# Reordering the end of the first attention stage and the start of the first product on TensorE

## Chip, cores, metric

One NeuronCore of one Trainium2 chip runs the whole program. The metric is the device time of one execution in microseconds (us).

## The reference

Attention over 8 batches, 12 heads, 448 tokens, head size 64, with normalised queries and keys; its output, viewed as 3584 rows of 768, goes through a two-layer product with a "snake" activation.

```python
def _attn_ref(q, k, v, g_q, g_k):
    q_n, k_n = rmsnorm(q, g_q), rmsnorm(k, g_k)
    # ... scale = 1 / sqrt(head size) ...
    scores = scale * np.matmul(q_n, k_n.transpose(0, 1, 3, 2))
    # ... softmax over the keys, which gives attn ...
    # ... attn times v is returned ...

def _moe_ref(x, w_in, w_out, alpha):
    h = x @ w_in                      # 768 -> 2048
    s = np.sin(alpha * h)
    g = h + s * s / (alpha + 1e-09)
    return g @ w_out                  # 2048 -> 768
```

## The kernel before

For each batch the kernel works through 6 pairs of heads in 3 chunks. A chunk has 7 score tiles (`scores`, one exponential each on ScalarE); a pair has 7 key tiles of values (`attend`), then a reciprocal on ScalarE (a logarithm and an exponential) and a division on VectorE that writes the pair's rows of `xT`. Then the first product makes 16 h tiles, each from 6 rows of weights, row `kt` needing pair `kt`'s division. From the second batch on, attention is interleaved with the second product of the batch before. The first batch has nothing to interleave with, so its waits are visible. The change touches only the end of that first stage.

PSUM, the memory that TensorE writes its results to, is given out as four pairs of banks. A new tile takes the pair that a predicted clock says comes free first, and waits for the last reader of what was in it. Fillers are matmuls on blank data whose results nobody uses:

```python
    def bank_pair(name, dtype=F32):
        slot = min(free_at, key=free_at.get)
        clock["pe"] = max(clock["pe"], free_at.pop(slot))
        ps = psum.tile([P, 2, 2048 // mybir.dt.size(dtype)], dtype, tag=f"ps{slot}", name=name)
        # ...
    def scores(c, j, warm=0):
        sc = bank_pair("sc")
        for _ in range(warm):                     # fillers on blank data
            nc.tensor.matmul(sc[:, 0], blank[:, :P], blank, start=True, stop=True)
        # ... 4 matmuls of 64*64 ...
        nc.scalar.activation(expT[c, j], sc[:, :, :S], ACT.Exp, scale=SCALE)

    def attend(pi, tiles=range(NJ)):
        if tiles[0] == 0:
            avs[pi] = bank_pair("av")
        # ... 4 matmuls of 64*64 for each key tile ...
        if tiles[-1] < NJ - 1:
            return
        nc.scalar.activation(rec, av[:, 1, :S], ACT.Ln)
        nc.scalar.activation(rec, rec, ACT.Exp, scale=-1.0)
        for hi in range(2):
            # ...
            nc.vector.tensor_mul(xT[b][r, hp, :], av[r, 0, :S], rec[o, :])

    def first_product(b, beside):
        # ...
        EARLY = 2
        tiles = {i: bank_pair("hps") for i in range(EARLY)}
        for kt in range(KT):
            for m in range(2 * EARLY):
                mm(tiles[m // 2], m, [kt])
        for i in range(MT // 2):
            if i >= EARLY:
                tiles[i] = bank_pair("hps")
                # ... 6 rows for each of 2 h tiles ...
            # ... snake of the two h tiles, then:
            for task in beside.get(i, ()):
                task()

    # end of the first stage; S_ = next score tile, A_ = values of the next pair (pairs 2 to 5 here)
    S_(1), A_(), S_(1), S_(1), S_(), A_(), S_()
    c4.reduce(0), c4.reduce(1)      # sums of squares of the fifth chunk, VectorE
    A_(2)                           # pairs 4 and 5, last key tiles last
    c4.rsqrt()
    # ... beside: c3.pe_transpose at 0, i.e. after the first two h tiles
    first_product(0, beside)
```

## Time and profile before

| | before |
|---|---|
| time, median of 3 | 436.57 us |
| span of the profiled execution | 434.7 us |
| TensorE busy | 98% |
| share of TensorE in the chain that ended last | 81% |
| first product of batch 0 starts | 39.05 us |
| its last 72 matmuls start | 45.18 us |

The waits and the timeline of the stretch are shown in the prediction. One line was not read closely enough before predicting. It is in the timeline of weight loads (start, length, engine, line, operation, operands, count, idle time before and its releaser) of the kernel before:

```profile
45.18 2.00 PEld L353 LDWEIGHTS <-w_in 128*128 128x128 bf16 x12
47.56 1.44 PEld L353 LDWEIGHTS <-w_in 128*128 128x128 bf16 x9 [0.38 <-DVE qkT L276]
```

In this trace weight loads run ahead of the matmuls, and a wait of theirs need not appear as idle matmul time: the second row has 0.38 us of it, the row of the 72 matmuls shows none. After 12 matmuls the load for the seventh h tile waits for VectorE's copy of the transposes, whose bank pair it inherits.

### The profile page before, as it was taken

The page shows a single profiled execution, that of the slowest core. Times are in us where ns is not written, and L with a number is a line of the kernel's source. Part 1 is how long each engine was busy: PE and PEld are TensorE (multiplying, and loading weights), DVE is VectorE, ACT ScalarE, POOL GpSimd, SP SyncE. Part 2 cuts the span into 40 slices and gives each one's busy share as a digit, 9 for nine tenths or more (in the row PEclk, how much of TensorE's full clock was granted, in tenths as well). Part 3 has the DMA queues.
Part 4 walks back from the last instruction along what each step waited for, and adds up shares of the span by engine and source line. Part 5 has one row for each costly group of instructions (what it writes and reads, how often), then busy time and mean ns, then how long its engine had stood idle before and what let it go on. Part 6 is the DMA issues. An engine that isn't in the chain of part 4 may idle for free.

```text
span 434.7 us, 9516 instructions
## 1 busy us (share of the span) xinstructions
PE 423.9 (98%) x3845; PEld 220.8 (51%) x3845; DVE 231.4 (53%) x335; ACT 338.5 (78%) x529; POOL 279.5 (64%) x263
## 2 busy tenths in 40 slices
PE   7889999999999999999999999999999999999996
PEld 3345554555455555555555555555555555555563
DVE  4787564557355564547454564464645474246511
ACT  5888789878888787878879788887878788788600
POOL 4968789936995559927798369946599176002300
PEclk9999999999999999999999999999999999999999
DMA  7999999691259704692067903494063901320022
GB/s 254 208 260 211 211 189 237 163 210 45 65 151 218 145 0 126 126 239 84 8 195 186 188 1 81 149 226 121 1 192 89 126 1 33 85 57 2 0 67 79
DMA packets 68240, 54.63 MB, mean 126 GB/s; under 512 B 39636, under 2 KB 63972, under 8 KB 68196
## 3 DMA queue, kind: packets, MB, share of 16 engines
q1 hardware_dynamic: 54834, 40.51, 36.6%
q0 software_dynamic: 12416, 11.81, 18.1%
q10 hardware_dynamic: 946, 1.70, 1.0%
q8 instruction: 30, 0.49, 0.5%
q14 instruction: 14, 0.11, 0.1%
HBM read 45.62 MB, written 11.01 MB: 130 GB/s over the span
## 4 chain that ended last, share of the span: by engine, by line
PE 81%; POOL 2%; DMA 1%; DVE 1%; issue 1%
PE ops L400 32%; PE hps L353 29%; PE av L314 13%; PE sc L294 7%; DMA qkT<-qkn 1%; POOL sq L221 1%; POOL qkn L246 1%; POOL qk L224 0%; DVE osb L406 0%; DVE xT L326 0%; DVE ms L227 0%
## 5 line engine op out<-in xcount | busy, mean ns | idle before, releaser
L297 ACT ACTIVATE expT<-sc 128x896 bf16<-128x896 f32 x168 | 144.6, 913 | 29.3 <-PE sc L294 28.3
L400 PE MATMUL ops<-w_out_sb,g_sb 128*128 128x384 bf16 x896 | 156.6, 327 | 0.0
L353 PE MATMUL hps<-xT,w_in 128*128 128x448 bf16 x768 | 147.3, 353 | 0.4 <-DVE xT L326 0.4
L335 POOL TENSOR_TENSOR s<-s 128x448 f32<-128x448 f32 x64 | 59.4, 932 | 115.0 <-ACT s L332 100.1
L400 PEld LDWEIGHTS <-g_sb 128*128 128x128 bf16 x896 | 83.1, 98 | 70.0 <-issue 18.8
L340 DVE SCALAR_TENSOR_TENSOR g_sb<-s,inv_alpha_sb,hps 128x448 bf16<-128x448 f32 x128 | 80.9, 677 | 62.1 <-POOL s L335 62.1
L353 PEld LDWEIGHTS <-w_in 128*128 128x128 bf16 x768 | 74.3, 98 | 72.3 <-issue 3.7
L332 ACT ACTIVATE s<-hps,alpha_sb 128x448 f32<-128x448 f32 x128 | 74.4, 627 | 28.9 <-PE hps L353 27.4
L326 DVE TENSOR_TENSOR xT<-av,rec 64x448 bf16<-64x448 f32 x96 | 59.7, 622 | 51.6 <-ACT rec L321 32.3
L246 POOL TENSOR_TENSOR qkn<-qk,inv 128x448 bf16<-128x448 f32 x80 | 72.6, 937 | 7.4 <-POOL qk L224 7.0
L221 POOL TENSOR_TENSOR sq<-qk 128x896 f32<-128x896 f32 x44 | 73.3, 1682 | 0.0
L314 PE MATMUL av<-expT,vb 64*64 64x448 bf16 x672 | 69.0, 349 | 1.2 <-ACT expT L297 0.8
L314 PE MATMUL av<-expT,ones 64*64 64x448 bf16 x672 | 69.1, 349 | 0.0
L227 DVE TENSOR_REDUCE ms<-sq 128x14 f32<-128x896 f32 x44 | 47.4, 1082 | 24.9 <-POOL sq L221 24.6
L406 DVE COPY osb<-ops 128x768 f32<-128x768 f32 (+1 forms) x33 | 27.6, 836 | 51.4 <-PE ops L400 45.5
L294 PE MATMUL sc<-qkT 64*64 64x448 bf16 x672 | 50.9, 361 | 1.7 <-DVE qkT L276 1.4
L224 POOL TENSOR_TENSOR qk<-qk,gg 128x896 f32<-128x896 f32 x24 | 50.1, 2090 | 1.7 <-ACT gg L171 1.7
L314 PEld LDWEIGHTS <-vb 64*64 64x64 bf16 x672 | 37.9, 107 | 13.4 <-issue 1.9
L314 PEld LDWEIGHTS <-ones 64*64 64x64 bf16 x672 | 37.1, 107 | 11.2
L337 ACT ACTIVATE s<-s 128x448 f32<-128x448 f32 x64 | 36.9, 577 | 2.7
L294 PEld LDWEIGHTS <-qkT 64*64 64x64 bf16 x672 | 14.9, 105 | 29.5 <-issue 26.2
L320 ACT ACTIVATE rec<-av 128x448 f32<-128x448 f32 x48 | 26.2, 545 | 4.0 <-PE av L314 3.5
(44 smaller groups left out, 140.8 us busy)
## 6 DMA issues: line engine op xcount, KB each, us to landing
qk<-in_q_dram SPq DMA_DIRECT2D x24, 448.0 KB, 4.3
qk<-in_k_dram SPq DMA_DIRECT2D x22, 448.0 KB, 5.2
out_dram<-osb SPq DMA_DIRECT2D x39, 192.0 KB, 2.8
vb<-in_v_dram POOLq DMA_DIRECT2D x32, 168.0 KB, 6.6
w_in<-in_moe_w_in_dram POOLq DMA_DIRECT2D x4, 768.0 KB, 11.8
w_out_sb<-in_moe_w_out_dram POOLq DMA_DIRECT2D x2, 1536.0 KB, 24.5
out_dram<-osb SPq DMA_DIRECT2D x26, 96.0 KB, 4.2
qk<-in_k_dram ACTq DMA_DIRECT2D x2, 448.0 KB, 5.9
```

Source lines behind the costliest of these rows:

```text
L221: nc.gpsimd.tensor_mul(st.sq[w], qk[ci][:, w], qk[ci][:, w])
L224: eng.tensor_mul(qk[ci][:, 0], qk[ci][:, 0], gg.to_broadcast([P, 2 * NJ, D]))
L246: eng.tensor_mul(n[:, :, hi, :], x[:, hi], inv[:, hi].unsqueeze(2).to_broadcast([P, NJ, D]))
L294: nc.tensor.matmul(sc[key_rows(pp, hi), pp, :S], qkt[r, 1, j * REST:(j + 1) * REST], qkt[r, 0, :], start=True, stop=True)
L297: nc.scalar.activation(expT[c, j], sc[:, :, :S], ACT.Exp, scale=SCALE)
L314: nc.tensor.matmul(av[o, part, :S], ones[r, :] if part else vb[b][r, hp, j, :], expT[pi // 2, j][r, pi % 2, :], start=(j == 0), stop=(j == ...
L326: nc.vector.tensor_mul(xT[b][r, hp, :], av[r, 0, :S], rec[o, :])
L332: nc.scalar.activation(s1, hps, ACT.Sin, scale=alpha_sb[:, m, :])
L335: nc.gpsimd.tensor_mul(s2, s1, s1)
L340: nc.vector.scalar_tensor_tensor(g_sb[:, m, (b % 2) * S:(b % 2 + 1) * S], s2, inv_alpha_sb[:, m, :], hps, op0=ALU.mult, op1=ALU.add)
L353: nc.tensor.matmul(ps[:, m % 2, :S], w_in_sb[m * 2 // MT][:, kt, m % (MT // 2) * P:(m % (MT // 2) + 1) * P], x[:, kt, :], start=(kt == 0), ...
L400: nc.tensor.matmul(st["ps"][:, k, :HALF], g_sb[:, m, c0:c0 + P], w_out_sb[:, m, half * HALF:(half + 1) * HALF], start=(m == 0), stop=(m == ...
```

## The change

Its intent is to remove TensorE's waits at the end of the stage: pair 3's reciprocal is held back so that the four last exponentials go first on ScalarE; the fifth chunk's sums leave the place in front of the last divisions; the first product does three rows of two h tiles before it needs a second bank pair, and puts the transposes where it would wait for the last division.

The diff, shortened (a helper that `A_(2)` used is dropped too):

```diff
         EARLY = 2
         tiles = {i: bank_pair("hps") for i in range(EARLY)}
-        for kt in range(KT):
+        for i in range(EARLY):
+            for m in (2 * i, 2 * i + 1):
+                mm(tiles[i], m, range(KT // 2))
+        for kt in range(KT // 2, KT):
+            if kt == KT - 1:
+                for task in beside.get(-1, ()):
+                    task()
             for m in range(2 * EARLY):
                 mm(tiles[m // 2], m, [kt])
@@
-    S_(1), A_(), S_(1), S_(1), S_(), A_(), S_()
+    S_(), A_()
     c4.reduce(0), c4.reduce(1)
-    A_(2)
+    attend(3, range(NJ - 1))
+    S_(), S_(), S_(), S_()
+    attend(3, [NJ - 1])
+    for last in (range(NJ - 1), [NJ - 1]):
+        for pi in (4, 5):
+            attend(pi, last)
     c4.rsqrt()
     beside = beside_h(0)
-    for i, task in ((0, lambda: c3.pe_transpose((0, 1))), (2, lambda: c4.scale(0, [0])), ...
+    for i, task in ((-1, lambda: c3.pe_transpose((0, 1))), (2, lambda: c4.scale(0, [0])), ...
```

More of the change, by code (lines that the diff above doesn't have):

```diff
@@ L472, in stage @@
         pairs = deque(b * NP + p for p in range(NP))
-        def values(n=1):
-            if n == 1:
-                return attend(pairs.popleft())
-            for js in (range(NJ - 1), [NJ - 1]):
-                for pi in list(pairs)[:n]:
-                    attend(pi, js)
-        return (lambda warm=0: scores(*tiles.popleft(), warm)), values
+        return (lambda warm=0: scores(*tiles.popleft(), warm)), (lambda: attend(pairs.popleft()))
     S_, A_ = stage(0)
@@ L521 @@
     load_qk(NC + 3)
-    S_(1), A_(), S_(1), S_(1), S_(), A_(), S_()
+    S_(), A_()
     c4.reduce(0), c4.reduce(1)
-    A_(2)
+    attend(3, range(NJ - 1))
[4 more added lines that the diff above has]
+            attend(pi, last)
     c4.rsqrt()
     beside = beside_h(0)
-    for i, task in ((0, lambda: c3.pe_transpose((0, 1))), (2, lambda: c4.scale(0, [0])), (3, lambda: c4.scale(0, [1])), (4, lambda: c4.scale(1, [0])),
+    for i, task in ((-1, lambda: c3.pe_transpose((0, 1))), (2, lambda: c4.scale(0, [0])), (3, lambda: c4.scale(0, [1])), (4, lambda: c4.scale(1, [0])),
                     (5, lambda: c4.scale(1, [1])), (6, step_of(NC + 1, 6)), (6, beside[3].pop())):
```

## The prediction

> **What bounds the kernel.** I read the page's busy shares and chain first, then the waits of TensorE between 25 and 46 us (the first batch's attention and the start of its first product), then the timelines of each engine there.
>
> ```profile
> PE 423.9 (98%) x3845; PEld 220.8 (51%) x3845; DVE 231.4 (53%) x335; ACT 338.5 (78%) x529; POOL 279.5 (64%) x263
> PEclk9999999999999999999999999999999999999999
> PE 81%; POOL 2%; DMA 1%; DVE 1%; issue 1%
> ```
>
> The matmul engine is busy in 98% of 434.7 us, at its full clock, and carries 81% of the chain that ended last. Only 10.8 us of it are idle, more than half of them before 35 us (29.1 busy of 35.0). The change touches a stretch of about 14 us that is executed once, so at best it can win the bubbles and the idle-time fillers of that stretch. These are the waits of TensorE there:
>
> ```profile
> PE sc L290 <- ACT expT L297: 1.1, 2, 0.8
> PE av L314 <- ACT expT L297: 0.6, 1, 0.6
> PE hps L353 <- DVE xT L326: 0.4, 1, 0.4
> ```
>
> The two last lie in the changed code. In the timeline (start, length, engine, line, operation, count, wait) they look so:
>
> ```profile
> 32.64 0.39 PE L290 MATMUL sc<-blank 128*128 128x512 bf16 x1
> ...
> 33.27 0.39 PE L290 MATMUL sc<-blank 128*128 128x512 bf16 x1
> ...
> 34.76 0.38 PE L314 MATMUL av<-expT,vb 64*64 64x448 bf16 x2 [0.59 <-ACT expT L297]
> ...
> 38.80 2.08 DVE L227 TENSOR_REDUCE ms<-sq 128x14 f32<-128x896 f32 x2
> ...
> 39.05 4.09 PE L353 MATMUL hps<-xT,w_in 128*128 128x448 bf16 x20
> ...
> 40.91 2.54 DVE L326 TENSOR_TENSOR xT<-av,rec 64x448 bf16<-64x448 f32 x4
> ...
> 43.51 0.92 PE L353 MATMUL hps<-xT,w_in 128*128 128x448 bf16 x4 [0.37 <-DVE xT L326]
> ...
> 44.36 0.89 PE L269 MATMUL tp<-ident,qkn 64*128 64x64 bf16 x28
> ...
> 45.18 13.91 PE L353 MATMUL hps<-xT,w_in 128*128 128x448 bf16 x72
> ```
>
> The reader sees fillers on blank data, a wait for an exponential, then the first product started at 39.05 with the operands of pairs 0 to 4. VectorE spends 2.08 us on the fifth chunk's sums just when the divisions of pairs 4 and 5 come due. The last pair's operand is ready at 43.45, so the last four matmuls of the first h tiles start at 43.51 instead of 42.91 (20 x 0.193 after 39.05): 0.60 us lost, of which the wait shows 0.37, the rest being drain. The transposes, ready since 33.4, stand behind them in the queue. From 45.18 to 66 us TensorE has no wait. So **45.18 is the mark**: how much earlier the 72 matmuls start is the gain.
>
> **What the Trainium skill says.** "TensorE: Matmul & The Clock Gate", section Back-to-back issue gap: N/2.4 + 2.5 ns, 189 ns for 448 columns; the trace has (13.91 - 0.35)/71 = 0.191, so it agrees. The same page, Part 2, step 1: only weight loads are pulled ahead, matmuls stay in program order; the transposes held up until 44.36 agree. "TensorEngine Tiling", Key Properties: "Changing tiling mode (not just tile) drains the TensorE"; going from 64*64 value matmuls to 128*128 ones costs 0.10 us here (the last value matmuls start at 38.76, their 0.19 end at 38.95, the next begins at 39.05), so it agrees. The clock page's table in "Why this matters for your kernels" allows no idle gaps over about 3 us; the stretch holds gaps up to 0.76 us at an unchanged clock, so shorter ones don't show it wrong.
>
> **The change part by part.** The instruction order of both kernels, laid side by side, differs in this stretch alone; afterwards only two PSUM bank pairs have exchanged names. TensorE loses three fillers (6 rows), everything else is moved. From the timeline I use: a key tile of values 0.19 (so 1.32 for seven, 1.13 for six), a tile of scores 0.19 to issue and 0.38 to finish, exponentials 0.90 alone and 0.82 in sequence, one logarithm plus exponential of a pair 1.1, one division 1.26 on VectorE, a semaphore 0.05. PSUM is given out as four pairs of banks, so a tile waits for the last reader of the pair that it inherits.
>
> Fillers. Each costs its 0.21 and two mode switches: from the end of the values at 32.51 to the scores at 32.96 are 0.45. The first (30.38) is worth nothing, as the values behind it wait until 31.19 for the second pair's division (29.88 + 1.26). The other two are 0.9 us of issue, but behind them stood the 0.59 wait for exponentials anyway.
>
> New order from 32.51, same until there. Six tiles of pair 3: 32.51 to 33.64. Scores 18 and 19: 33.64 to 34.02. ScalarE has finished pair 2's reciprocal and starts exponential 18 at 34.10 (scores done 34.02, 0.08 later), to 35.00; score tile 20 needs the same bank pair, so **it waits until 35.05**: about 1 us of new stall (0.85 visible). Score tile 21 needs the bank pair of pair 2, which VectorE frees at 35.20: 35.25. Exponentials 19, 20, 21 end at about 35.78, 36.60, 37.42. Last tile of pair 3: to 35.63. Pair 4 starts when exponential 19 frees its bank pair, 35.83; five tiles to 36.77, its sixth to 36.96; six of pair 5, 38.09; the two last tiles, 38.47. With the 0.10 switch the first product starts at **38.57 rather than 39.05: 0.48 earlier**.
>
> The chain of the divisions. Pair 3's logarithm is now behind exponential 21 on ScalarE: it starts at 37.40, reciprocal ready 38.55 (before: 37.48, so **1.07 later**). Pair 4's values finish at 38.44, reciprocal 39.65; pair 5's 40.69. The sums on VectorE now run at 35.20 to 36.27 and, since GpSimd's second square ends at 36.60, 36.65 to 37.72: in idle time. Divisions: pair 3 38.58 to 39.84, pair 4 to 41.10, pair 5 to **42.37, before 43.45**.
>
> First product. Six matmuls of h tiles 0, 1: 38.57 to 39.73. The bank pair of tiles 2, 3 is the one pair 3's values held, freed at 39.84; its weight load carries this wait, so about 40.0 (**0.27 of new stall**). Six more: 41.16. Key row 3 for four tiles 41.93, row 4 42.70 (pair 4 ready at 41.10). Transposes in front of the last row, 0.90 with both switches as before: 43.60. Last row, operand ready since 42.37: 44.37. The 72 matmuls start at **44.37 in place of 45.18: 0.81 earlier**. Check: 0.48 from the earlier start, plus 0.60 of removed wait, less 0.27 of new wait = 0.81.
>
> What follows. The first sine comes only 0.1 us earlier (last row at 43.60 against 43.51), so GpSimd, which had no gap from 46.45 to 52.65, can't follow at once; but TensorE asks for a bank pair of the first sines only at 44.37 + 4.6 = 49.0, and these are free at about 47. GpSimd has waits of 0.44 again from 53.09 and catches up. In steady state the pairs of h tiles cost TensorE 2.27 us, ScalarE 1.75, GpSimd 1.87: TensorE stays the bound and the 0.81 passes on. Loads bound to absolute time: the second product's weights land some 22 and 27 us after issues at 32.1 and 39.0, that is 54 and 66, needed at 58.9 and (the 49th matmul) 70.1 before, 58.1 and 69.3 after. The chunk transposed by DMA lands near 67 and is needed at 69.35, then 68.5. All have over 2 us of room. Total: 436.57 - 0.81 = **435.76**.
>
> **The rivals.** (a) *A wait takes the place of the one removed, and all is eaten*: the bank pairs. Four score tiles in a row share three of them, and pair 3 holds the fourth. For: the order of waits shows them, and I already charge 1.0 and 0.27 for them. Against all of it being lost: 0.60 at the end of the division chain goes by the 2.08 of sums taken from in front of it. If ScalarE runs 0.4 us later than I have it, pair 4's start, and pair 3's division with its bank pair, slip by as much: 436.2. (b) *Nothing counts since the stage later waits on something else* (the snake on GpSimd, or the loads): 436.5. Against: no wait of TensorE from 45.18 to 66 and the margins above. (c) *Without fillers the clock drops*: some 3 us at half speed would cost 1 to 2 us, 437.5 to 438. The gaps stay about 1 us, so unlikely. (d) *More gain than counted*: if the weight load's wait at h tiles 2, 3 is hidden and the exponential starts sooner, 435.4.
>
> **Range and chances.** My sum is made of measured durations, and its error is mainly semaphore and queue delays of 0.05 to 0.1 at some five handovers: +-0.3. Rivals (a) and (b) weigh more on the slow side. Three runs of before spread 0.06 us. Range 435.3 to 436.3. Two per cent would be 8.7 us, ten times the change: within 2% is all but certain.
>
> **What would show it.** Right: no blank matmuls after 30; a wait of scores for the exponential of about 0.85 ending near 35.05; the sums at 35.2 to 37.7; pair 3's division later (38.6) but pair 5's done near 42.4; the first product starting near 38.6 with a small stop near 39.8; transposes near 42.8 ahead of the last row; 72 matmuls from about 44.4; the second product from 58.1. Wrong: those starting at 45 or later, a clock under 1.00 near 35, new TensorE waits for g tiles or weights between 45 and 72, or a gain present at 58 us and gone by the end.

## The result

| | before | after |
|---|---|---|
| median (4 runs each) | 436.60 us | 435.39 us |
| lowest | 436.56 us | 435.29 us |
| ratio | | 0.9971, 95% interval 0.9954 to 0.9988 |

A ratio is the mean time of one kernel's runs over the mean of the other's of the same rounds, so it is not quite the ratio of the medians. The change is within 2%, and a gain: 1.2 us by the medians, 1.04 us by the two profiled executions (436.51 and 435.47). A second set of six runs later gave 435.29 against 436.48, ratio 0.9973 (0.9959 to 0.9988).

The waits of TensorE between 25 and 46 us in the kernel after (total us, times, longest):

```profile
PE sc L294 <- ACT expT L297: 1.2, 2, 0.8
PE sc L290 <- ACT expT L297: 0.8, 1, 0.8
PE av L314 <- DVE xT L326: 0.4, 1, 0.4
```

The wait for `xT` in front of the last row is gone. A score tile now waits 0.83 us for an exponential instead of values waiting 0.59. These are the timelines of VectorE and TensorE in the kernel after:

```profile
35.31 2.08 DVE L227 TENSOR_REDUCE ms<-sq 128x14 f32<-128x896 f32 x2
38.58 3.83 DVE L326 TENSOR_TENSOR xT<-av,rec 64x448 bf16<-64x448 f32 x6 [1.19 <-ACT rec L321]
```

```profile
35.13 0.59 PE L294 MATMUL sc<-qkT 64*64 64x448 bf16 x8 [0.83 <-ACT expT L297]
...
38.71 4.01 PE L353 MATMUL hps<-xT,w_in 128*128 128x448 bf16 x20
42.65 0.89 PE L269 MATMUL tp<-ident,qkn 64*128 64x64 bf16 x28
43.47 14.55 PE L353 MATMUL hps<-xT,w_in 128*128 128x448 bf16 x76
```

The sums run at 35.3 to 37.4 in idle time (in one piece, not in two up to 37.7 as predicted: GpSimd's work in front of its squares began at 29.68 in this execution and at 30.64 in that of before), the last division ends at 42.4 (38.58 + 3.83) instead of 43.45, and from 38.71 to the second product TensorE has no visible wait. The reader can check the steps of the prediction here: 35.05, 38.57, 42.37 and 42.8 were its times for the stall's end, the product's start, the last division and the transposes.

**A yardstick.** The two executions differ by 0.08 to 0.09 us before the changed code is reached (a score tile starts at 28.77 and at 28.86), and by 0.08 when pair 2's values start (31.19 and 31.27). From here on I measure each trace from the first value matmul of pair 2 to the first matmul of the second product: **27.74 us before (31.19 to 58.93), 26.59 after (31.27 to 57.86): 1.15 us gained.** From there to the end of the span every kernel needs 375.8 us (375.76 to 375.86), so nothing is given back or won later.

### The profile page after: what moved, and what is told of

The parts are those of the page before. It is cut to its first block, busy times and chain, and to the rows that moved or that the text cites. A ratio compares the mean times of both kernels' runs of the same rounds, so it can differ in the third digit from the quotient of the medians.

```text
span 433.7 us, 9510 instructions
## 1 busy us (share of the span) xinstructions
PE 423.0 (98%) x3842; PEld 220.7 (51%) x3842; DVE 231.5 (53%) x335; ACT 338.6 (78%) x529; POOL 279.7 (64%) x263
## 4 chain that ended last, share of the span: by engine, by line
PE 81%; POOL 2%; DMA 1%; DVE 1%; issue 1%
PE ops L406 32%; PE hps L353 29%; PE av L314 13%; PE sc L294 7%; DMA qkT<-qkn 1%; POOL sq L221 1%; POOL qkn L246 1%; POOL qk L224 0%; DVE osb L412 0%; DVE xT L326 0%; DVE ms L227 0%
## 5 line engine op out<-in xcount | busy, mean ns | idle before, releaser
L314 PEld LDWEIGHTS <-vb 64*64 64x64 bf16 x672 | 37.7, 107 | 12.9 <-issue 1.7
```

Source lines behind the costliest of these rows:

```text
L314: nc.tensor.matmul(av[o, part, :S], ones[r, :] if part else vb[b][r, hp, j, :], expT[pi // 2, j][r, pi % 2, :], start=(j == 0), stop=(j == ...
```

## The experiments

The theory: TensorE's time is set by two hand-over chains, exponentials on ScalarE up to the start of the product, and divisions on VectorE up to its last row; the parts of the change act on these and don't simply add. Rival 1: the fillers and the new score order are the gain. Rival 2: the moved sums are. Rival 3: each part adds its own. "Stretch" is the yardstick; "lowest" is compared with the lowest of before in the same rounds.

| kernel | stretch, us | against before | lowest (before) | ratio |
|---|---|---|---|---|
| before | 27.74 | | | |
| after, first and second time | 26.59, 26.59 | -1.15 | 435.25 (436.35) | 0.9973 |
| sums alone | 27.08 | -0.66 | 435.68 (436.34) | 0.9979 |
| product alone | 27.09 | -0.65 | 435.76 (436.34) | 0.9983 |
| sums and product | 26.96 | -0.78 | 435.70 (436.35) | 0.9986 |
| order alone | 28.73 | +0.99 | 437.36 (436.39) | 1.0019 |
| after without sums | 28.08 | +0.34 | 436.80 (436.34) | 1.0010 |
| after without groups | 27.34 | -0.40 | 436.02 (436.34) | 0.9984 |
| before without fillers | 27.74 | 0.00 | 436.44 (436.39) | 0.9997 |
| after with fillers back | 27.05 | -0.69 | 435.77 (436.35) | 0.9985 |
| after, transposes late | 26.71 | -1.03 | 435.36 (436.39) | 0.9973 |
| after, pair 3 whole | 27.59 | -0.15 | 436.31 (436.35) | 1.0010 |
| after, transposes in the stall | 26.22 | -1.52 | 434.92 (436.39) | 0.9951 |

All were correct, all timed in five rounds. The differences of the stretches and those of the lowest times agree within 0.13 us.

### Sums alone

```diff
-    S_(1), A_(), S_(1), S_(1), S_(), A_(), S_()
-    c4.reduce(0), c4.reduce(1)
+    S_(1), A_()
+    c4.reduce(0), c4.reduce(1)
+    S_(1), S_(1), S_(), A_(), S_()
     A_(2)
```

> Kernel before with one part alone: the fifth chunk's sums moved from in front of the last two pairs' divisions to behind the second pair's on VectorE. My theory (the end of the division chain holds the last four matmuls of the first h tiles): last division done near 42.65 instead of 43.45, the last row starts without a wait near 42.8, and the 72 matmuls start near 44.6 instead of 45.18, so 0.6 us faster than before. Rival 1 (the fillers and the new order of scores are the whole gain): nothing, within 0.15. Rival 2 (the sums are the whole gain, everything else is decoration): the whole 1.05 us.

Measured: 435.91 against 436.54, stretch -0.66. The divisions of the last two pairs on VectorE, then TensorE in this kernel:

```profile
40.25 2.55 DVE L326 TENSOR_TENSOR xT<-av,rec 64x448 bf16<-64x448 f32 x4 [1.40 <-ACT rec L321]
```

```profile
39.12 4.71 PE L353 MATMUL hps<-xT,w_in 128*128 128x448 bf16 x24
```

They end at 42.80, and all 24 early matmuls run in one piece. The theory holds; both rivals that expected 0 or 1.05 fall.

### The change without its sums

```diff
     S_(), A_()
-    c4.reduce(0), c4.reduce(1)
     attend(3, range(NJ - 1))
     S_(), S_(), S_(), S_()
     attend(3, [NJ - 1])
+    c4.reduce(0), c4.reduce(1)
```

> Kernel after with the sums put back in front of the last two pairs' divisions. My theory: pair 3's division comes later in the new order (38.5 to 39.8), the sums follow to 41.9, pair 4's division ends at 43.1 and pair 5's at 44.4; the fifth row of the first product waits until 43.2, the 72 matmuls start near 45.7, so the kernel is 0.4 to 0.6 us SLOWER than before: the new order can't live without the moved sums. Rival 1 (the order of scores and no fillers are the gain): about 1.05 us faster than before, as the kernel after. Rival 2 (sums are the whole gain): equal to before.

Measured: 436.84 against 436.54, stretch +0.34. TensorE in this kernel:

```profile
38.62 3.25 PE L353 MATMUL hps<-xT,w_in 128*128 128x448 bf16 x16
43.20 0.92 PE L353 MATMUL hps<-xT,w_in 128*128 128x448 bf16 x4 [1.33 <-DVE xT L326]
```

The product starts just as early as in the kernel after, then its fifth row waits until 43.20, as expected. A loss of 0.46 by the lowest times, in the range of 0.4 to 0.6, and of 0.34 by the stretch, a little under it; the 0.12 us of the copies, told further down, are won in this kernel too.

### Product alone

On the kernel before, the first hunk of the change and the place of the transposes:

```diff
-        for kt in range(KT):
+        for i in range(EARLY):
+            for m in (2 * i, 2 * i + 1):
+                mm(tiles[i], m, range(KT // 2))
+        for kt in range(KT // 2, KT):
+            # ... tasks of -1 ahead of the last row ...
-    for i, task in ((0, lambda: c3.pe_transpose((0, 1))), ...
+    for i, task in ((-1, lambda: c3.pe_transpose((0, 1))), ...
```

> Kernel before with the new first product alone (first rows of two h tiles by themselves, transposes ahead of the last row). My theory: the transposes fill the 0.6 us wait for the last division, the last row starts near 43.9 and the 72 matmuls near 44.7, plus 0.1 for a bank pair freed earlier by the copies: 0.5 to 0.6 us faster than before. It removes the same wait as the moved sums, so the two don't add. Rival 1 and 2: nothing. Rival 3 (parts add up independently, a third each): 0.35 us.

Measured: 435.89 against 436.54, stretch -0.65. TensorE in this kernel:

```profile
43.13 0.89 PE L269 MATMUL tp<-ident,qkn 64*128 64x64 bf16 x28
```

It goes from the fifth row to the transposes at 43.13 and from these to the last row at 43.95. The wait for the last division is unchanged on VectorE; the transposes lie in it.

### Sums and product together

Both diffs above, on the kernel before.

> Kernel before with both parts that gained alone: sums moved and the new first product, old order of scores. My theory: both remove the same wait of 0.6 to 0.7 us, so together they give hardly more than one: 0.65 to 0.8 us faster than before (27.7 less 0.7 from pair 2's first value matmul to the second product). Rival (parts add): 1.3 us.

Measured: stretch -0.78, 435.86 against 436.48. Not 1.31: the two parts remove the same wait, so the second one adds 0.12. Rival 3 falls.

### Order alone

```diff
-    S_(1), A_(), S_(1), S_(1), S_(), A_(), S_()
+    S_(), A_()
+    attend(3, range(NJ - 1))
+    S_(), S_(), S_(), S_()
+    attend(3, [NJ - 1])
     c4.reduce(0), c4.reduce(1)
-    A_(2)
+    # ... pairs 4 and 5 as in A_(2) ...
```

> Kernel before with the new order of scores and values alone (fillers gone, pair 3 split, four score tiles in a row); sums and first product as before. My theory: the start of the first product moves 0.42 us ahead as in the kernel after, but pair 3's division is late, so the third h tile stops TensorE near 39.0 for 0.8 us, the sums push the last divisions to 43.1 and 44.4, and the 72 matmuls start near 46.2: 0.9 to 1.1 us SLOWER than before. Rival 1 (new order and fewer fillers are the gain): 0.4 to 1.1 us faster.

Measured: stretch +0.99, lowest 437.36 against 436.39. TensorE in this kernel, h tiles from 38.61:

```profile
39.80 2.82 PE L353 MATMUL hps<-xT,w_in 128*128 128x448 bf16 x14 [0.64 <-DVE xT L326]
43.19 0.92 PE L353 MATMUL hps<-xT,w_in 128*128 128x448 bf16 x4 [0.57 <-DVE xT L326]
44.48 0.92 PE L353 MATMUL hps<-xT,w_in 128*128 128x448 bf16 x4 [0.37 <-DVE xT L326]
```

The product starts 0.42 earlier and then stops three times for divisions. The part that looks like the core of the change is a loss of 1 us without the other two, and a gain of 0.37 with them (27.74 - 0.78 against 26.59). Rival 1 falls.

### Without groups

```diff
-        for i in range(EARLY):
-            for m in (2 * i, 2 * i + 1):
-                mm(tiles[i], m, range(KT // 2))
-        for kt in range(KT // 2, KT):
+        for kt in range(KT):
```

> Kernel after, but the first rows again row by row over four h tiles (transposes still ahead of the last row). My theory: the third and fourth h tile need the bank pair that pair 3's division frees only at 39.8, so row by row TensorE stops after two matmuls at about 39.0 for 0.8 us; the 72 matmuls start near 45.1: only 0.1 to 0.3 us faster than before, 0.8 us slower than after. Rival (the grouping only tidies up): as fast as after, 1.05 us faster than before.

Measured: 436.20 against 436.54, stretch -0.40, so 0.75 slower than after. TensorE in this kernel:

```profile
38.74 0.55 PE L353 MATMUL hps<-xT,w_in 128*128 128x448 bf16 x2
39.92 3.58 PE L353 MATMUL hps<-xT,w_in 128*128 128x448 bf16 x18 [0.64 <-DVE xT L326]
```

The new order frees pair 3's bank pair only with its late division, and the third h tile wants that pair. The groups put four more matmuls of the first two h tiles (rows 1 and 2) into this time. They exist to repair what the order breaks.

### Before without fillers, and the change with fillers

In the kernel before, then in the kernel after:

```diff
-    S_(1), A_(), S_(1), S_(1), S_(), A_(), S_()
+    S_(), A_(), S_(), S_(), S_(), A_(), S_()
```

```diff
-    S_(), A_()
+    S_(1), A_()
     # ...
-    S_(), S_(), S_(), S_()
+    S_(1), S_(1), S_(), S_()
```

> Kernel before with the three fillers taken out and nothing else. My theory: ScalarE paces this part, the values of pair 3 still wait for the same exponential near 34.75, so the first product starts at the same time: 0 (within 0.1 us); TensorE only shows about 0.9 us more waiting, the clock stays at full speed. Rival 1: TensorE has three times up to 0.45 us less to do, so 0.4 to 1.3 us faster. Rival (the clock drops without fillers): slower by 1 us or more.

> Kernel after with the three fillers put back at their score tiles (17, 18, 19). My theory: here nothing stands behind them any more that waits anyway; the fillers at tiles 18 and 19 push exponential 18 back by about 0.4 us and with it everything up to the first product: 0.35 to 0.45 us slower than after, 0.65 to 0.75 faster than before. So the same fillers cost nothing in the old order and 0.4 in the new one. Rival (fillers run in time that is idle in both orders): equal to after.

Measured: 0.00 in the old order (27.74), 0.46 slower than after in the new one (27.05 against 26.59). The waits of TensorE in the kernel before without fillers say why:

```profile
PE av L314 <- ACT expT L297: 0.9, 1, 0.9
```

The wait of 0.59 for the exponential has become 0.9, and the values start when they did. In the new order score tile 18, which follows a filler, starts the chain of four exponentials. ScalarE in the kernel after, then in the kernel after with fillers:

```profile
34.16 3.35 ACT L297 ACTIVATE expT<-sc 128x896 bf16<-128x896 f32 x4 [0.17 <-PE sc L294]
```

```profile
34.51 3.35 ACT L297 ACTIVATE expT<-sc 128x896 bf16<-128x896 f32 x4 [0.62 <-PE sc L294]
```

Its wait for the tile grows from 0.17 to 0.62, and the chain starts 0.46 later in the stretch (3.35 instead of 2.89 us after pair 2's first value matmul).

In the profiled executions of the two kernels without these fillers (before without fillers, and after) the clock row reads 9 (90% or more) in all forty slices, and the mean granted clock is 0.999 in both: there the fillers were not needed to hold the clock. Over all executions this is not shown. Before without fillers had a mean of 0.995 in four of six, which were 0.77 to 0.94 us longer (its median is 437.27, against 436.85); before had 0.995 or less in three of eleven in the same rounds. The kernel after, also without these fillers, was under 0.997 in one of ten. Over all kernels it is 16 of 52 executions without these fillers and 9 of 57 with them that read 0.996 or less, on several chips, which does not settle it. The one fall of the clock that was traced (next section) lies ahead of the place of these fillers.

### Transposes late

```diff
-    for i, task in ((-1, lambda: c3.pe_transpose((0, 1))), ...
+    for i, task in ((0, lambda: c3.pe_transpose((0, 1))), ...
```

> Kernel after with the transposes back behind the first h tiles. My theory: in the kernel after the last division (42.4) is no longer awaited, so the place of the transposes is not worth anything any more for TensorE: the 72 matmuls (76 less 4) start at the same time, the kernel is equal to after within 0.15 us (1.0 faster than before), the first sine starts about 0.7 us earlier. Rival (transposes ahead of the last row are what removed the wait): 0.5 us or more slower than after.

Measured: stretch 26.71, 0.12 slower than after; lowest 435.36. The 24 early matmuls run without them and the sines start earlier, but the 72 that follow take 13.75 us to the second product as they did before, 0.12 more than without a wait. That is the bank pair of the copies: at 47.91 a weight load of this kernel has waited 0.38 for them, as in the kernel before. Its median of 436.13 is not comparable, as four of its six executions were long. The profiled one had a slow start. TensorE's start-up fillers in the profiled execution of this kernel, then in that of the kernel after; this code is the same in both:

```profile
6.77 5.21 PE L199 MATMUL ps<-blank 128*128 128x512 bf16 x15
```

```profile
6.57 3.41 PE L199 MATMUL ps<-blank 128*128 128x512 bf16 x15
```

Fifteen equal matmuls took 5.21 us instead of 3.41, and pair 2's values start at 32.57 instead of 31.27. This is one source of long executions. The profiled execution of "pair 3 whole", the next kernel, shows another. Its fifteen fillers took 3.41 us, but this is its clock row:

```profile
PEclk9989999999999999999999999999999999999999
```

Read in steps of 1 us, the granted clock was 0.81 from 21 to 22 us, 0.50 from 22 to 25 and 0.98 from 25 to 26, ahead of all changed code and after no TensorE wait over 0.9 us since the first matmul. From pair 0's first value matmul to the next filler took 2.71 us there and 1.45 in the kernel after.

The record gives the mean granted clock of 109 executions. In 25 it is 0.996 or less, and every one of these is 0.55 to 2.41 us above the lowest of its kernel and rounds. Of the other 84, ten are 1.45 to 1.73 above (the one with the slow start is at 1.48), and 74 at most 0.46. Only two of the long ones were profiled, so what happened in the others is not shown. The kernel before has both kinds, which is why I compare lowest times and the stretch.

### Pair 3 whole

```diff
-    attend(3, range(NJ - 1))
+    attend(3)
     S_(), S_(), S_(), S_()
-    attend(3, [NJ - 1])
# and, so that pair 4 is not given pair 3's banks:
-        give_back(avs.pop(pi), passes(0.0, 1.06) + 1.4)
+        give_back(avs.pop(pi), passes(0.0, 1.06) + (6.0 if pi == 3 else 1.4))
```

> Kernel after, but pair 3's values whole, with its reciprocal on ScalarE ahead of the four exponentials (its bank pair's predicted return put off, so that no later tile is given it early). My theory: the reciprocal takes 1.06 us of ScalarE in front of exponential 18, all four exponentials, pairs 4 and 5 and the first product come about 1.0 us later: the second product starts 0.9 us later than in after, only 0.1 to 0.3 us faster than before. Rival (ScalarE has room, holding back the last key tile is worth nothing): equal to after.

Measured: stretch 27.59, 1.00 slower than after. ScalarE in this kernel (here everything starts 0.62 us later than in the kernel after):

```profile
34.79 0.54 ACT L320 ACTIVATE rec<-av 128x448 f32<-128x448 f32 x1 [0.19 <-PE av L314]
35.85 3.32 ACT L297 ACTIVATE expT<-sc 128x896 bf16<-128x896 f32 x4
```

The reciprocal takes 1.06 us ahead of the exponentials (34.79 to 35.85), and everything behind comes that much later. In the kernel after the four exponentials start at 34.16, which is 1.07 us earlier in the stretch. One held-back key tile of 0.19 us is worth 1.0 us because it decides the order on another engine.

### Transposes in the stall: a version that beats both

```diff
     S_(), A_()
-    c4.reduce(0), c4.reduce(1)
-    attend(3, range(NJ - 1))
-    S_(), S_(), S_(), S_()
+    S_(), S_()
+    c3.pe_transpose((0, 1))
+    attend(3, range(3))
+    S_()
+    attend(3, range(3, NJ - 1))
+    c4.reduce(0), c4.reduce(1)
+    S_()
     attend(3, [NJ - 1])
-    for last in (range(NJ - 1), [NJ - 1]):
-        for pi in (4, 5):
-            attend(pi, last)
+    attend(4), attend(5)
     # ...
-    for i, task in ((-1, lambda: c3.pe_transpose((0, 1))), (2, lambda: c4.scale(0, [0])), ...
+    for i, task in ((2, lambda: c4.scale(0, [0])), ...
```

> An attempt to beat both: kernel after with the transposes moved further ahead, to behind score tiles 18 and 19, where TensorE otherwise stands still for 1 us for exponential 18; three tiles of pair 3, one score tile, three tiles, one score tile, the last tile; pairs 4 and 5 whole. If the remaining stall of 1 us at the four score tiles is real loss, the first product starts later by 0.6 us but with no transposes in it, and the second product starts about 0.5 us before that of the kernel after: 1.5 to 1.6 us faster than before. If the stall is hidden anyway (ScalarE or the divisions set the end): equal to after or slower.

Measured: 435.02 against 436.85 in the same rounds, ratio 0.9951 (0.9931 to 0.9970), lowest 434.92, stretch 26.22: 0.37 better than after where about 0.5 was expected. TensorE in this kernel:

```profile
33.41 0.88 PE L269 MATMUL tp<-ident,qkn 64*128 64x64 bf16 x28 [0.35 <-DVE qkn L246]
34.73 0.38 PE L314 MATMUL av<-expT,vb 64*64 64x448 bf16 x2 [0.45 <-ACT expT L297]
...
39.21 18.34 PE L353 MATMUL hps<-xT,w_in 128*128 128x448 bf16 x96
```

The first product now has all its 96 matmuls in one piece. It starts 0.61 later in the stretch (8.05 us after pair 2's first value matmul, 7.44 in the kernel after) and takes 18.17 us to the second product instead of 19.15, so 0.37 is won. Part of the 0.83 us stall was thus real loss. It is not all won, as the transposes wait 0.35 for their input and the next values 0.45 for an exponential. The edit moves the sums and the values too, and no run separates these from the transposes. This one is quicker than the kernel after by 0.33 us in the lowest times (434.92 and 435.25, from different rounds) and by 0.37 in the stretch. That the two differ by as much in time can be told only from these, as the intervals of the ratios overlap.

## Why the prediction was right, and where its sum was off

The measured median lies in the range of 435.3 to 436.3, near its edge: a gain of 1.15 where 0.81 stood. Point by point:

- **The bound and the mark**: the bound is right: the stretch's difference passes to the end of the span unchanged, in thirteen kernels. The mark catches most: the last 72 matmuls start at 44.23 (43.47 + 4 x 0.1893), 1.03 earlier in the stretch, and 0.12 of the gain lies behind it (see "Left out").
- **Fillers worth nothing in the old order**: right, 0.00. That the new order no longer tolerates them (0.46) was not said.
- **New stall of 0.85 us ending at 35.05**: 0.83, ending at 35.13 with 0.08 of later start. Right.
- **Start of the product 0.48 earlier**: 0.42 (7.86 to 7.44 us after pair 2's first value matmul). Right within 0.06.
- **Removed wait of 0.60**: mis-sized, 0.67. I took 0.193 us for a matmul, which is 13.91/72: this counts the drain of the last one and a hidden wait. 76 matmuls in 14.55 us give (14.55 - 0.35)/75 = 0.1893, so the 20 early ones of the kernel before should have ended at 42.84, not 42.91.
- **New stall of 0.27 at the third h tile**: the term that failed most: 0.06. Twenty unhindered matmuls need 19 x 0.1893 + 0.35 = 3.95; they took 4.01. I had added about 0.10 for the weight load after its wait, and let the product start at 38.57, not 38.71. The load did wait, but past the sixth matmul only for little, and its own time showed little in the matmuls. This is its line in the timeline of weight loads of the kernel after:

```profile
39.89 2.38 PEld L353 LDWEIGHTS <-w_in 128*128 128x128 bf16 x14 [0.32 <-DVE xT L326]
```

Six matmuls after 38.71 end at 39.85, so the load came only 0.04 late.
- **Left out**: the wait for the transposes' copies. "From 45.18 to 66 us TensorE has no wait" was read from matmul rows alone. The 72 matmuls of the kernel before took 13.75 us to the second product; 72 x 0.1893 are 13.63. The 0.12 go when the transposes come earlier, and come back in the kernel with late transposes (26.71).

Corrected sum: 0.42 + 0.67 - 0.06 + 0.12 = 1.15, the measured stretch. The terms are read from the same two traces as the stretch, so that they close proves little; the 0.12 alone has runs of its own (late transposes, and sums and product against sums alone).

- **Rivals**: (a) occurred in part, as the stalls of 0.83 and 0.06, and ate nothing like all. (b) did not occur, and (c) not in the profiled execution (mean granted clock 0.999). That the clock could fall after waits of under 1 us, as in the execution of "pair 3 whole", was not foreseen. (d) named the weight load and 435.4, and the median is 435.39. Its weight load came true; its sooner exponential did not (34.16, with 0.08 of later start in it, where 34.10 was predicted), and it had neither the 0.12 nor the larger removed wait, so that its figure fits so well is partly luck.

What stays open: why the start-up fillers take 3.4 us in one execution and 5.2 in another, and why the granted clock falls in some; no run varied either.

## What to carry to other kernels

When an engine is the bound, put its instruction order beside the hand-overs that it waits for, and ask of each moved instruction which other engine's queue it reorders: here one key tile moved a logarithm behind four exponentials. Parts of a change that remove the same wait don't add, and a part can be a loss until another one repairs what it delays (here a bank pair and a division), so don't judge such parts one at a time. Measure gains of 0.3% between two marks inside the trace when executions differ by more in code that was not touched.

## What the Trainium skill lacked or had wrong

- "TensorE: Matmul & The Clock Gate", Back-to-back issue gap: the formula N/2.4 + 2.5, which the section gives for isolated matmuls (an estimate of 189 ns for 448 columns), fits a stream of weight load and matmul pairs here, 0.1893 us over 76 of them. The same section says that such streams come to about 131 ns at 512 columns and that the formula over-counts there; no run here shows that, and 0.1893 at 448 columns speaks against it.
- The same page, Part 1: it puts the start of full speed at about 4 us into the matmuls, give or take 500 ns, with 426.7 against 215.7 ns for a 512-column matmul; another note there counts 6, 11 or 14 slow matmuls in executions of one kernel. Here the same 15 such matmuls took 3.41 or 5.21 us, on average 0.23 or 0.35 each. The first ten of the 11 fillers before them were slow in both executions; in the second, eight or nine of the 15 were slow as well, up to about 10.2 us, which is 9 us after the first matmul at 1.20. The profile's granted clock reads 1.00 in both, so it does not show this.
- "TensorEngine Tiling", Key Properties: says that a change of tiling mode drains TensorE, without a figure. Here 0.10 us passed between 64*64 and 128*128 matmuls (38.95 to 39.05).
- No page that I read says how a wait that stands on a weight load shows up: the two here cost 0.06 and 0.12 us of matmul time, while the rows of matmuls show no idle time and the rows of weight loads show 0.32 and 0.38.
